# One block's residual added by GpSimd's accumulating DMAs, its norm's statistics on VectorE, and a new instruction order

## The chip, the cores and the metric

The kernel runs on one NeuronCore of a Trainium2 chip. The metric is the device time of one execution in microseconds. The profile names the engines PE (TensorE matmul), PEld (TensorE weight load), ACT (ScalarE), DVE (VectorE), POOL (GpSimd) and SP (SyncE, which only issues DMAs).

## The reference

The input is one sequence of S = 2048 positions with D = 448 features in bf16. Two layers with pre-norm residuals follow each other.

```
x = A_x
h  = x + A(layernorm(x))         # A: 16 heads of 28; each position attends to itself and
                                 #    positions 2, 4, ... 14 before it (8 taps, dilation 2), then @ wo
h2 = h + B(layernorm(h))         # B, called with y = layernorm(h):
                                 #   g  = gelu(layernorm(y) @ w1), its four 112-column groups shifted by -1, +1, -2, +2 positions
                                 #   x1 = y + g_shifted @ w2
                                 #   B  = x1 + gelu(layernorm(x1) @ w3) @ w4          # w3: 448 x 1792
```

All layer norms are without weights: (x - mean) / sqrt(var + eps).

## The kernel before, in words

The sequence is cut into 4 blocks of 512 positions (t = 0 to 3) of 4 tiles of 128 positions each. Everything stays on chip; `xin` holds the input tiles and later the sum h. The steps of a block are phases: N1 (norm of x: statistics by `bn_stats` and `bn_aggr`, a logarithm and an exponential for the power, normalization, and a small copy that doubles the last 64 columns), A1 (transposes, and q and k projections, evicted to `arena`), V (v projection to `vt`, and GpSimd DMAs that gather windows of it into `vw`), A2 (products of q and shifted k on VectorE into `qk_r`, summed by matmuls), S (softmax on VectorE and ScalarE, transposes of `pb`), A3 (VectorE spreads the weights into `bd_r`, matmuls with `vw`), O (projection with `wo`, plus the residual, into `xin`), B1 (norm of h), M (projection with w1 and GELU). The rest runs in five units u of 3, 4, 4, 4 and 1 tiles: B2 (w2 and residual), T (norm, and on GpSimd an fp32 add of `xin` to the running sum), W3 (w3 and GELU, into `h3T`), B3 (w4, last adds, output DMA from `ost`).

**The residual of O** is chosen per block by RESIDUAL (line 62, used in `phase_A3`). With 't', a fifth matmul with the identity adds the tile of `xin` in PSUM and ScalarE copies the result to `xin`; with 'v', VectorE adds PSUM to `xin`. Where STATS["B1"] (line 16) of a block is 'a', ScalarE's copy sums the row as well, and `sums_stats` has ScalarE square the four tiles; where it is 'v', `ln_stats` runs `bn_stats` and `bn_aggr` on VectorE. Block 2 (the third) has 't' and 'a'. With 'a' the identity matmul is used whatever RESIDUAL says.

**The order.** The phases first make a list of operations with their dependencies. ORDER (lines 21 to 59) is an order of all of them, written out; `schedule` (line 259) walks it. An engine's instructions are issued in the order in which they stand in ORDER, and an engine waits at a semaphore where an operation needs the result of another engine. `schedule` also has a model of times; with ORDER given, that model picks buffer slots, inserts filler matmuls into long gaps, and decides which GpSimd DMAs and which DMA transposes wait for each other. Operations marked `block` are VectorE instructions that the model holds to collide with GpSimd's.

Buffers are pools of slots: 8 PSUM banks, 2 of `qk_r`, 3 of `ost`; a new user of a slot waits for the old ones. `contract` groups projections so that the half-row matmuls of several outputs run in pairs; a pool "win" with one slot keeps these groups apart in the model.

Of the kernel before, what the change touches and what calls it, by code (L numbers as in the profile page):

```python
# [5 lines left out]
ACT = mybir.ActivationFunctionType  # L6
ALU = mybir.AluOpType
# [8 lines left out]
STATS = {'N1': 'vvva', 'B1': 'vvav', 'B2': 'aaaaa'}  # L16
# [43 lines left out]
RUNS = {'A3': '1111', 'W3': '23334'}  # L60
LOADS = '01'
RESIDUAL = 'ttvv'
# [126 lines left out]
class _Sched:  # L189
# [69 lines left out]
    def schedule(self, dma_bw=240.0, dma_fixed=2000.0, table_load=1300.0):  # L259
# [18 lines left out]
        blocked = held = entry = 0.0; waiting = None  # L278
        assert sorted(ORDER) == list(range(n))
        for idx in ORDER:  # L280
# [45 lines left out]
            else:  # L326
# [3 lines left out]
                if op.eng == "pool":  # L330
                    waiting = op if blocked > st else None
                    st = entry = max(st, blocked)
                    if op.block:
                        held = st + dur
                elif op.block:
                    if waiting is not None and st <= entry + 50.0:
                        late = st + dur - entry
                        free["pool"] += late; waiting.t1 += late; entry += late
                        for ch in children[waiting.idx]:
                            if waiting in ch.deps:  # L340
                                rdy[ch.idx] = max(rdy[ch.idx], waiting.t1 - (self.OWN if ch.eng == "pool" else 0.0))
                        if waiting.block:
                            held += late
                    else:
                        st = max(st, held)
                    blocked = st + dur
# [67 lines left out]
def bass_sequential_preLN__sliding_local_dilated__mixer_s_mlp__prompt_kernel(  # L414
# [17 lines left out]
    EPS = 1e-5  # L432
# [15 lines left out]
    with ExitStack() as es:  # L448
# [41 lines left out]
        P_win = _Pool("win", None, 1)  # L490
# [110 lines left out]
        def rstd(kind, i, m=4, summed=False, norm="v", how="p"):  # L601
# [15 lines left out]
            if how == "a":  # L617
                first = int(kind == 1)
                if not summed and (norm == "a" or kind == 1):
                    dve("tensor_scalar", 4, ns=78.0, out=nm[:, kind, i:i + m], in0=mv[:, kind, i:i + m, 0], scalar1=-1.0, scalar2=None, op0=ALU.mult)  # L620
# [511 lines left out]
```

## Time and profile before

| | us |
|---|---|
| median of 3 runs (199.99 to 200.40) | 200.25 |
| the profiled execution | 199.96 |
| span of its profile, first to last instruction | 198.2 |
| PE busy | 189.7 |
| ACT busy | 143.4 |
| DVE busy | 121.7 |
| POOL busy | 46.0 |

The span leaves out 1.76 us of the profiled execution's own time. Busy times of engines overlap, since the engines run beside each other; the granted TensorE clock was 1.00 throughout. Nearly all instructions carry one line number (that of the loop that emits them, L1090), so they are told apart by the tiles they write and read.

### The profile page before, as it was taken

The numbers are of one execution on the slowest core, as the hardware profiler recorded it, in microseconds if no ns is written. First come the engines' busy times: TensorE is split into PE (matmuls) and PEld (weight loads), VectorE is DVE, ScalarE is ACT, GpSimd is POOL, SyncE is SP. The second block draws the span as 40 slices with busy tenths as digits, with TensorE's granted clock in tenths as the row PEclk, the third lists the DMA queues.
The fourth block names the chain that finished last, engine by engine and source line by source line (L and its number), as shares of the span: only waits on it lengthen the run. The fifth ranks groups of instructions, "written<-read, shape, count | busy, mean of one in ns | idle before, by whom it ended". The sixth has DMA issues, their size and how long they took to land.

```text
span 198.2 us, 4119 instructions
## 1 busy us (share of the span) xinstructions
PE 189.7 (96%) x1667; PEld 92.6 (47%) x1667; DVE 121.7 (61%) x222; ACT 143.4 (72%) x321; POOL 46.0 (23%) x96
## 2 busy tenths in 40 slices
PE   6899999889999989999989999999999999999994
PEld 2555333443454545544545444455444455446753
DVE  5888889999989999947957775101314052310024
ACT  4849986997999999997589699991345961645300
POOL 6540199003500000036040204302050000760000
PEclk9999999999999999999999999999999999999999
DMA  5950579943995000055410410009300023210003
GB/s 160 326 162 3 107 179 224 189 88 58 237 286 198 5 3 3 10 107 126 86 20 0 80 31 3 23 0 202 102 26 0 2 40 66 73 46 0 3 0 116
DMA packets 24467, 16.81 MB, mean 85 GB/s; under 512 B 17824, under 2 KB 22880, under 8 KB 24448
## 3 DMA queue, kind: packets, MB, share of 16 engines
q1 hardware_dynamic: 22368, 9.24, 19.7%
q0 software_dynamic: 2080, 7.31, 14.8%
q8 instruction: 13, 0.21, 0.4%
q14 instruction: 6, 0.05, 0.1%
HBM read 7.91 MB, written 1.84 MB: 49 GB/s over the span
## 4 chain that ended last, share of the span: by engine, by line
PE 62%; ACT 19%; DVE 8%; DMA 5%; POOL 4%; issue 1%; SPq 0%
PE ps L1090 62%; ACT arena L1090 5%; ACT actT L1090 5%; ACT vt L1090 3%; DMA vw<-vt 3%; ACT lntm L1090 2%; DVE qk_r L1090 2%; DMA xin<-in_A_x_dram 1%; DVE lntm L1090 1%; POOL w_s L1090 1%; POOL vw L1090 1%; DVE arena L1090 1%; ACT xin L1090 1%; POOL wo_s L1090 1%; ACT L1085 1%
## 5 line engine op out<-in xcount | busy, mean ns | idle before, releaser
L1090 PE MATMUL ps<-actT,arena 128*128 128x512 bf16 (+6 forms) x404 | 71.5, 344 | 0.3 <-ACT actT L1090 0.2
L1090 PEld LDWEIGHTS ps<-actT,arena 128*128 128x128 bf16 (+1 forms) x404 | 30.7, 97 | 37.4 <-issue 6.7
L1090 PE MATMUL ps<-arena,h3T 128*128 128x448 bf16 (+1 forms) x238 | 46.4, 342 | 0.0
L1090 ACT ACTIVATE h3T<-ps 128x512 bf16<-128x512 f32 (+1 forms) x60 | 30.6, 578 | 14.0 <-PE ps L1090 13.8
L1090 ACT ACTIVATE arena<-ps 128x512 bf16<-128x512 f32 (+5 forms) x64 | 32.0, 524 | 12.0 <-PE ps L1090 11.5
L1090 DVE SCALAR_TENSOR_TENSOR ost<-ps,mrs,arena 128x448 bf16<-128x448 f32 (+1 forms) x17 | 10.9, 654 | 37.8 <-PE ps L1090 35.7
L1090 DVE TENSOR_TENSOR qk_r<-arena 128x4096 bf16<-128x4096 bf16 (+1 forms) x16 | 31.8, 2016 | 2.8 <-PE ps L1090 2.8
L1090 PEld LDWEIGHTS ps<-arena,h3T 128*128 128x128 bf16 x238 | 22.6, 98 | 19.3 <-issue 0.5
L1090 POOL DMA_DIRECT2D vw<-vt x15 | 9.0, 605 | 48.9 <-DMA actT<-lntm 48.4
L1090 DVE TENSOR_TENSOR bd_r<-arena,bmask 80x2048 bf16<-80x2048 bf16 x16 | 18.7, 1214 | 2.2 <-ACT arena L1090 2.2
L1090 POOL TENSOR_TENSOR arena<-arena,xin 128x448 f32<-128x448 f32 x16 | 16.3, 1037 | 15.2 <-ACT lntm L1090 14.5
L1090 ACT ACTIVATE actT<-ps 128x512 bf16<-128x512 f32 (+2 forms) x27 | 17.8, 679 | 2.6 <-PE ps L1090 2.4
L1090 ACT ACTIVATE lntm<-arena,nm 128x448 bf16<-128x448 f32 x16 | 10.6, 662 | 8.6 <-DVE nm L1090 8.6
L1090 POOL TENSOR_TENSOR rs_y<-rs_x,mhalf 128x4 f32<-128x4 f32 (+1 forms) x5 | 4.7, 934 | 50.1 <-DVE rs_x L1090 50.1
L1090 PE MATMUL ps<-wo_s,actT 128*128 128x448 bf16 x64 | 14.5, 354 | 1.7 <-ACT actT L1090 1.6
L1090 DVE BATCH_NORM_STATS2 st<-xin 128x6 f32<-128x448 bf16 x24 | 13.8, 610 | 1.7 <-DMA xin<-in_A_x_dram 1.6
L1090 PE MATMUL ps<-actT,w_s 128*112 128x512 bf16 (+1 forms) x64 | 14.5, 387 | 0.0
L1090 DVE SCALAR_TENSOR_TENSOR arena<-xin,rs_y,ps 128x448 f32<-128x448 bf16 x16 | 10.4, 677 | 6.7 <-PE ps L1090 6.6
L1090 PE MATMUL ps<-w_s,arena 112*128 112x448 bf16 x64 | 13.6, 352 | 0.3 <-ACT arena L1090 0.3
L1090 PE MATMUL ps<-arena,actT 128*128 128x448 bf16 (+1 forms) x64 | 12.3, 353 | 0.5 <-ACT arena L1090 0.5
L1090 PEld LDWEIGHTS ps<-actT,w_s 128*112 128x112 bf16 (+1 forms) x64 | 6.5, 128 | 6.1 <-issue 2.0
L1090 PEld LDWEIGHTS ps<-w_s,arena 112*128 112x128 bf16 x64 | 6.0, 98 | 6.3 <-ACT arena L1090 1.1
(73 smaller groups left out, 190.4 us busy)
## 6 DMA issues: line engine op xcount, KB each, us to landing
out_dram<-ost SPq DMA_DIRECT2D x15, 112.0 KB, 1.7
arena<-in_B_w_dram POOLq DMA_DIRECT2D x1, 1568.0 KB, 15.2
arena<-in_B_w_dram POOLq DMA_DIRECT2D x1, 1344.0 KB, 10.4
vw<-vt POOLq DMA_DIRECT2D x4, 320.0 KB, 5.3
vw<-vt POOLq DMA_DIRECT2D x4, 256.0 KB, 5.2
xin<-in_A_x_dram SPq DMA_DIRECT2D x2, 448.0 KB, 5.8
xin<-in_A_x_dram SPq DMA_DIRECT2D x3, 224.0 KB, 5.0
arena<-in_A_wqkv_dram SPq DMA_DIRECT2D x1, 672.0 KB, 4.8
```

The source lines that it names most:

```text
L1085: eng.preload_act_table_set("natural_log_exp_and_others")
L1090: inst = getattr(eng, meth)(**kw)
```

## The change

Four things change:
- Block 2 gets RESIDUAL 'd' and STATS 'v'. ScalarE copies the projection from PSUM to a slot of `ost` in bf16, and GpSimd issues a DMA that adds the slot to the tile of `xin`, once per tile. The identity matmul goes, ScalarE's row sums and squares go, and VectorE computes the block's statistics from `xin`.
- ORDER is replaced by another list over all operations (1104 instead of 1096).
- In `schedule` the model's DMA rate goes from 240 to 215; operations marked `block` on VectorE and GpSimd now depend on each other for real (a semaphore wait for the last such operation of the other engine, in the order of the list). More of VectorE's small instructions are marked: the shifts `nm`, the inputs `rs_x` of the powers, and the doubling copies.
- The pool "win" gets 3 slots instead of 1.

```diff
-STATS = {'N1': 'vvva', 'B1': 'vvav', 'B2': 'aaaaa'}
+STATS = {'N1': 'vvva', 'B1': 'vvvv', 'B2': 'aaaaa'}
...
-    0, 9, 8, 10, 1, 2, 3, 11, 6, 4, 35, 22, 36, 5, 37, 12, 23, 38, 13, 24, 14, 25, 39, 15, 26, 46, 16, 40, 27, 52, 17, 28, 41, 18, 53, 29, 47, 60,
-    19, 48, 30, 42, 49, 54, 20, 55, 31, 61, 66, 56, 62, 43, 21, 32, 63, 57, 67, 33, 50, 34, 68, 44, 51, 69, 64, 58, 104, 70, 105, 65, 45, 106, 107,
-    59, 72, 112, 71, 108, 73, 109, 110, 111, 144, 74, 113, 114, 75, 115, 142, 116, 122, 76, 117, 145, 124, 143, 77, 120, 78, 118, 148, 123, 79, 80,
...
+    0, 9, 7, 6, 8, 10, 1, 2, 3, 11, 4, 35, 22, 36, 37, 12, 23, 38, 13, 24, 14, 25, 39, 15, 26, 46, 16, 27, 52, 17, 28, 18, 53, 29, 55, 56, 19, 30,
+    66, 60, 20, 31, 21, 32, 61, 67, 47, 48, 33, 54, 34, 49, 50, 51, 57, 58, 62, 63, 68, 104, 105, 106, 69, 59, 64, 108, 65, 40, 107, 111, 142, 112,
+    109, 110, 70, 41, 113, 114, 42, 144, 145, 143, 71, 43, 116, 146, 115, 117, 122, 120, 148, 44, 124, 147, 149, 45, 150, 118, 125, 123, 72, 151, 73,
...
-RESIDUAL = 'ttvv'
+RESIDUAL = 'ttdv'
...
-    def schedule(self, dma_bw=240.0, dma_fixed=2000.0, table_load=1300.0):
+    def schedule(self, dma_bw=215.0, dma_fixed=2000.0, table_load=1300.0):
...
                 if op.eng == "pool":
-                    waiting = op if blocked > st else None
-                    st = entry = max(st, blocked)
                     if op.block:
-                        held = st + dur
+                        waiting = None
+                        if guard["dve"]:
+                            op.deps.add(guard["dve"]); st = max(st, guard["dve"].t1)
+                        guard["pool"] = op
+                    else:
+                        waiting = op if blocked > st else None
+                        st = entry = max(st, blocked)
                 elif op.block:
+                    if guard["pool"]:
+                        op.deps.add(guard["pool"]); st = max(st, guard["pool"].t1)
+                    guard["dve"] = op
...
-        P_win = _Pool("win", None, 1)
+        P_win = _Pool("win", None, 3)
...
-                on_pe = RESIDUAL[t] == "t" or STATS["B1"][t] == "a"
+                by_dma = RESIDUAL[t] == "d"
+                on_pe = not by_dma and (RESIDUAL[t] == "t" or STATS["B1"][t] == "a")
...
-                if on_pe:
+                if by_dma:
+                    o = _Tile(P_o)
+                    act(o(), b(lambda v: v[:, 0:D]), ACT.Copy, D)
+                    dma(lambda o=o: "res%d" % o.slot, xin[:, i, :], o(), 128 * D * 2, 600.0, "pool", accum_op=ALU.add)
+                elif on_pe:
                     act(xin[:, i, :], b(lambda v: v[:, 0:D]), ACT.Copy, D, **kw)
```

The numbers of the lists that matter at the start: block 0's tiles 0, 1, 2 and 3 have their statistics in 46, 52, 60, 66 and their aggregates in 47, 53, 61, 67; the logarithms and exponentials are 48 and 49, 55 and 56, 62 and 63, 68 and 69; tile 1's shift is 54 and 57; the normalizations are 50, 58 (on ScalarE), 64, 70 and the doubling copies 51, 59, 65, 71; the transposes of the four tiles are 104, 108, 112, 116, with filler matmuls 105, 106, 109, 110, 113, 114 between. 118 to 125 are block 0's first projections on half the width, 189 is a projection of V, 142 to 149 are the statistics and aggregates of block 1's tiles and 204 and 206 its transposes. In the new list 204 and 206 stand behind six of the projections 118 to 125 and 189; in the old list 204 stands behind all of block 0's projections.

On GpSimd's queue the new list has the four loads of wo ahead of every gather of `vw`, a load of w3 in two parts (202, 203) ahead of two of block 0's three gathers, and block 3's four gathers ahead of the four adding DMAs, without block 1's DMA transpose before them. In block 3's part of the list, the row maximum and the subtraction of its softmax (S 3) stand ahead of block 2's four normalizations, and the new statistics between the products of A2 3.

More of the change, by code (lines that the diff above doesn't have):

```diff
@@ L277, in schedule @@
         table = None
-        blocked = held = entry = 0.0; waiting = None
+        blocked = entry = 0.0; waiting = None; guard = dict(dve=None, pool=None)
         assert sorted(ORDER) == list(range(n))
@@ L341, in schedule @@
                                 rdy[ch.idx] = max(rdy[ch.idx], waiting.t1 - (self.OWN if ch.eng == "pool" else 0.0))
[L342 to L345, printed above, removed]
                     blocked = st + dur
@@ L530, in dma @@
         def dma(chan, out_ap, in_ap, nbytes, dur=450.0, eng="sp", behind=(), **kw):
-            op = S.add(eng, "dma_start", dur, 1000.0 if eng == "pool" else 0.0 if not callable(chan) else -1300.0, chan=chan, nbytes=nbytes, out=out_ap, in_=in_ap, **kw)
+            op = S.add(eng, "dma_start", dur + 100.0 * (eng == "pool"), 1000.0 if eng == "pool" else 0.0 if not callable(chan) else -1300.0, chan=chan, nbytes=nbytes, out=out_ap, in_=in_ap, **kw)
             op.odeps.update(behind)
@@ L596, in sums_stats @@
             lo, m = tiles[0], len(tiles)
-            dve("tensor_scalar", 4, ns=78.0, out=nm[:, kind, lo:lo + m], in0=mv[:, kind, lo:lo + m, 0], scalar1=-1.0 / D, scalar2=None, op0=ALU.mult)
+            dve("tensor_scalar", 4, ns=78.0, block=True, out=nm[:, kind, lo:lo + m], in0=mv[:, kind, lo:lo + m, 0], scalar1=-1.0 / D, scalar2=None, op0=ALU.mult)
             for n, i in enumerate(tiles):
@@ L619, in rstd @@
                 if not summed and (norm == "a" or kind == 1):
-                    dve("tensor_scalar", 4, ns=78.0, out=nm[:, kind, i:i + m], in0=mv[:, kind, i:i + m, 0], scalar1=-1.0, scalar2=None, op0=ALU.mult)
+                    dve("tensor_scalar", 4, ns=78.0, block=True, out=nm[:, kind, i:i + m], in0=mv[:, kind, i:i + m, 0], scalar1=-1.0, scalar2=None, op0=ALU.mult)
                 power_act(first)
@@ L629, in rstd @@
             if not summed and (norm == "a" or kind == 1):
-                dve("tensor_scalar", 4, ns=78.0, out=nm[:, kind, i:i + m], in0=mv[:, kind, i:i + m, 0], scalar1=-1.0, scalar2=None, op0=ALU.mult)
+                dve("tensor_scalar", 4, ns=78.0, block=True, out=nm[:, kind, i:i + m], in0=mv[:, kind, i:i + m, 0], scalar1=-1.0, scalar2=None, op0=ALU.mult)
             if kind == 1:
-                dve("tensor_scalar", 4, ns=78.0, out=rs_x[:, kind, 1, i:i + m], in0=var, scalar1=by * (1.0 + EPS), scalar2=EPS * EPS,
+                dve("tensor_scalar", 4, ns=78.0, block=True, out=rs_x[:, kind, 1, i:i + m], in0=var, scalar1=by * (1.0 + EPS), scalar2=EPS * EPS,
                     op0=ALU.mult, op1=ALU.add)
@@ L635, in rstd @@
             elif summed:
-                dve("tensor_scalar", 4, ns=78.0, out=rs_x[:, kind, 0, i:i + m], in0=var, scalar1=by, scalar2=EPS, op0=ALU.mult, op1=ALU.add)
+                dve("tensor_scalar", 4, ns=78.0, block=True, out=rs_x[:, kind, 0, i:i + m], in0=var, scalar1=by, scalar2=EPS, op0=ALU.mult, op1=ALU.add)
             else:
-                dve("tensor_scalar", 4, ns=78.0, out=rs_x[:, kind, 0, i:i + m], in0=var, scalar1=EPS, scalar2=None, op0=ALU.add)
+                dve("tensor_scalar", 4, ns=78.0, block=True, out=rs_x[:, kind, 0, i:i + m], in0=var, scalar1=EPS, scalar2=None, op0=ALU.add)
             if kind == 1:
@@ L641, in rstd @@
                     shifts(1)
-                dve("tensor_scalar", 4, ns=78.0, out=rs_x[:, kind, 0, i:i + m], in0=var, scalar1=by, scalar2=EPS, op0=ALU.mult, op1=ALU.add)
+                dve("tensor_scalar", 4, ns=78.0, block=True, out=rs_x[:, kind, 0, i:i + m], in0=var, scalar1=by, scalar2=EPS, op0=ALU.mult, op1=ALU.add)
             power(0)
@@ L674, in doubled @@
         def doubled(ln, lo, n):
-            dve("tensor_copy", 64, ns=142.0, out=ln(lambda v: v[:, lo:lo + n, D:512]), in_=ln(lambda v: v[:, lo:lo + n, 384:D]))
+            dve("tensor_copy", 64, ns=142.0, block=True, out=ln(lambda v: v[:, lo:lo + n, D:512]), in_=ln(lambda v: v[:, lo:lo + n, 384:D]))
         def transposed(ln, how, n=4, w=2):
```

71 rows, old and new, of the table ORDER are left out of this document.

## The prediction, made blind

> **What bounds the kernel now.** I read the page first, then the windows of 5 us, the chain of waits in order of time, TensorE's own waits, and the timeline of the first 20 us.
>
> ```profile
> PE 189.7 (96%) x1667; PEld 92.6 (47%) x1667; DVE 121.7 (61%) x222; ACT 143.4 (72%) x321; POOL 46.0 (23%) x96
> ```
>
> TensorE is busy for 189.7 of 198.2 us. It starts at 1.59 us, and its last matmul ends 2.5 us before the span does; so only 4.4 us of idle time lie inside its work. The windows (length, busy time of PE, PEld, DVE, ACT, POOL) show where:
>
> ```profile
> 5.00:10.00 5.00, 4.30 (x36) 2.59 (x35) 4.37 (x17) 4.28 (x12) 2.57 (x11) 1.00 1.09 323
> 10.00:15.00 5.00, 5.00 (x40) 2.92 (x38) 4.40 (x13) 2.49 (x8) 1.93 (x15) 1.00 0.52 156
> ...
> 35.00:40.00 5.00, 4.48 (x52) 2.18 (x53) 5.00 (x5) 4.89 (x13) 0.00 (x0) 1.00 1.02 185
> 40.00:45.00 5.00, 3.88 (x144) 2.10 (x137) 5.00 (x5) 4.86 (x13) 0.00 (x0) 1.00 0.48 95
> ...
> 70.00:75.00 5.00, 4.43 (x83) 2.02 (x81) 4.96 (x9) 4.91 (x14) 0.00 (x0) 1.00 0.01 3
> ...
> 85.00:90.00 5.00, 4.96 (x43) 2.40 (x42) 2.23 (x2) 5.00 (x16) 2.35 (x4) 1.00 0.56 104
> ...
> 100.00:105.00 5.00, 4.21 (x28) 2.14 (x27) 2.69 (x5) 4.95 (x16) 2.33 (x4) 1.00 0.00 0
> ```
>
> Idle PE: 0.70 before the first transposes, 1.64 from 35 to 45, 1.2 between 60 and 80, 0.79 at 101. Between 10 and 35 and from 105 on there is none. VectorE is nearly full from 30 to 85, ScalarE from 60 to 90: in the first half three engines run close together. The chain:
>
> ```profile
> 6.77 10.68 PE ps L1090 x88
> ...
> 87.94 3.43 DVE qk_r L1090 x2
> ...
> 100.96 0.70 DVE pb L1090
> ...
> 101.71 93.95 PE ps L1090 x664
> ```
>
> So the third block's norm lies in a stage that ends on VectorE (87.94 to 101.66), and after it TensorE alone counts. The start, which the new ORDER rearranges:
>
> ```profile
> 4.09 0.25 DVE L1090 BATCH_NORM_AGGREGATE mv<-st 128x2 f32<-128x6 f32 x2
> 4.64 0.63 DVE L1090 BATCH_NORM_STATS2 st<-xin 128x6 f32<-128x448 bf16 x1 [0.30 <-DMA xin<-in_A_x_dram]
> 6.13 0.36 DVE L1090 TENSOR_SCALAR lntm<-xin,mv,rs_y 128x448 bf16<-128x448 bf16 x1
> 6.77 0.40 PE L1090 MATMUL ps<-ident,lntm 128*128 128x128 bf16 x4 [0.70 <-DVE lntm L1090]
> 8.80 0.39 PE L1090 MATMUL ps<-ident,lntm 128*128 128x128 bf16 x4
> 9.02 5.80 PE L1090 MATMUL ps<-actT,arena 128*128 128x256 bf16 x40
> 13.61 0.21 DVE L1090 COPY lntm<-lntm 128x256 bf16<-128x256 bf16 x1
> 14.65 0.61 PE L1090 MATMUL ps<-ident,lntm 128*128 128x128 bf16 x8
> ```
>
> First transposes 6.77, fourth tile's 8.80, block 0's projections from 9.02, block 1's transposes 14.65, with no gap from 7.46 on.
>
> **Part 1, TensorE.** Four identity matmuls of 448 columns go. In the dense run at 129.27 us, 49 such matmuls take 9.43; without the last one's drain of some 0.35 that is 0.19 each: -0.76. All lie on the path. Walking both lists by the matmuls' tiling mode gives 85 changes of mode before and 86 after. One costs about 0.19: 18 full and 6 paired half matmuls at 121.48 take 4.91, where 21 x 0.216 is 4.53, for two changes. Net -0.57.
>
> **Part 2, ScalarE and VectorE.** ScalarE loses four squares (86.24 to 90.6; 0.65 apart) and eight accumulator reads of 0.20 to 0.25, about 4 us. It does not end that stage, so I count nothing. VectorE gains four statistics of 0.59 and four aggregates of some 0.12, 2.8 us. They go between the products for block 3, where VectorE waited 2.47 us for TensorE before 87.94. That idle time hides them: 0; without it, +2.8 on the VectorE chain.
>
> **Part 3, the transfers.** Four issues of 0.6 us each on GpSimd's queue (vw rows), which stood idle for 35.1 us until 87.37. Behind them on it are the norm's powers and the fp32 adds, some 10 us later. How long an adding transfer takes no row shows. Bounds: 1.7 us (112 KB to DRAM) and 5.8 (median of vw, queued); I take 3, nearer the first in size and with little else in flight. The next reader, the statistics, stands after two products of 2.3 us and block 1's norm, so up to 5.8 is hidden. Nearer is the buffer: ost has three slots, so the fourth copy on ScalarE waits for the first transfer. Between the first and the fourth copy stand one residual copy, two of actT, two of transposes and two more copies, about 4.4 us; issue and landing need 3.6. Cost 0, at the upper end +2. Just ahead of them the queue now has block 3's four window transfers, which before waited for a transpose until 87.37; their 656 KB may still be in flight, which is why 5.8 stays the bound. By the Trainium skill (DMA: Bandwidth & Descriptors, Anatomy of one DMA) a GpSimd transfer takes about 2.0 us plus bytes over 436 GB/s, an estimate of 2.3 here; by it the sum would be the same.
>
> **Part 4, explicit waits between GpSimd's adds and VectorE's small steps.** Beside two adds at 92.57 one normalization took 1.11 instead of 0.39 and one nm 0.99 instead of 0.17: the stall of 0.7 to 0.8 is there already. A semaphore in its place: 0, from -0.8 to +1.0 (one add). Queued behind a waiting VectorE step are the products and softmax steps of block 3; TensorE waits for those.
>
> **Part 5, the order at the start.** This is the term that decides. The new list puts tile 0's aggregate behind the statistics of tiles 3 and 2. They start at 4.64 with the transfer; two at 0.59, three aggregates at 0.12: 6.2 us. Logarithm and exponential (0.53) give 6.75, the normalization starts at 6.8 instead of 6.13, the first transposes at 7.4 (+0.65). ScalarE then does tile 1's shift and normalization (0.28 + 0.74) before tile 2's power: tile 2 transposes at 8.75, its fillers last until 9.8. VectorE puts a statistic of block 1 before tile 3's normalization, and another with two aggregates before its copy: 8.7 + 0.57 + 0.36 + 0.57 + 0.25 + 0.18 = 10.6, transposes at 10.7 instead of 8.80. The projections stand behind them on TensorE. Next the new list has only 18 narrow projections and one group of V (2.5 us) ahead of block 1's transposes, where the old had 5.6. TensorE reaches them at 13.5, but block 1's norm is ready at about 14.4: from 10.65, two statistics and aggregates 1.4, powers 0.53, four normalizations 1.3 to 1.6, copy 0.21. So at the same moment (14.4 against 14.65) TensorE has done 3.1 us less work: +2.8. The groups' evictions follow: the half-row matmuls that close block 0's groups end near 16.8 instead of 12.7, so ScalarE and VectorE are late too, by 2 to 3 us. On GpSimd's queue two of block 0's three window transfers move behind two parts of w3 (1.1 us of issue, 458 KB) and one transfer of block 1; their landing at 38.3 becomes 39 to 40, which the late softmax of block 0 covers; without that cover it costs 1.5.
>
> **Part 6, what gives it back.** TensorE can absorb delay only where it waited: 1.64 + 1.2 + 0.79 = 3.6 us. At 47.81 its wait ended on a transfer that does not move, worth about 1.0. The new list runs block 3's softmax ahead of block 2's normalizations, so the 0.79 at 101 should shrink, but its chain on VectorE starts late. I take 1.5 back; ends 0.5 and 3.5.
>
> **Part 7, the tail.** From block 2's projection on, the two lists hold 96.1 and 96.15 us of matmul and mode time: 0. Block 3's projection stands 2.1 us nearer to its norm, whose normalizations now precede unit 2's; 0, at worst +1.
>
> **Sum.** On the profiled execution, 199.96 (span 198.2 and 1.76 around it): -0.57 + 2.8 - 1.5 = +0.7, 200.7. The median shown is 0.29 above it: 201.0.
>
> **Rivals.**
> *The start is swallowed (faster).* All 3.5 us of later waits take up the 2.8 and the rest; -0.57 - 0.7 gives 199.0, with half of it 199.9. For: DVE and ACT have 1.3 and 2.1 us of idle time from 20 to 35. It decides if A1 3 starts before 49 us. Against: DVE stands at 4.8 to 5.0 of 5 from 30 to 85. Chance 0.30, of it 0.20 for faster.
> *Nothing is given back.* VectorE's lag of over 2 us reaches the softmax of block 3, and the new statistics lie on it: 200.25 - 0.57 + 2.8 = 202.5, with part of the 2.8 of part 2 up to 203. It decides when VectorE no longer waits before the third product of A2 3. Chance 0.09.
> *The adding transfers are slow.* Over 4 us each, the fourth copy blocks ScalarE by 2 us where it is 4.9 of 5 full: 203. Chance 0.06.
> *The clock falls back.* The first warm-up matmuls start 0.43 us apart, the later ones 0.22. TensorE's gap before the first transposes grows from 0.7 to 1.4, with two of 0.9 after it; should the slow pace return for 3.4 us, half of that is lost: 202.7. Chance 0.05. The Trainium skill (TensorE: Matmul & The Clock Gate, Part 1) has the clock halve after an idle window of about 3.4 us; by that rule these gaps are too short.
>
> **How the numbers follow.** Forecast 0.50, of it 0.04 within 0.2% of 200.25 (0.4 us, about what a measurement of this kernel can tell); swallowed start 0.20 faster and 0.10 the same; the other three 0.20 slower. That makes 0.20, 0.14 and 0.66. The forecast's own range is 200.4 to 202.0; the range to 199.0 and 203.2 takes in the first two rivals.
>
> **What would show it.** Right: first transposes near 7.4, tile 3's near 10.7, a TensorE wait before block 1's at 14.4; A1 3 at 50 to 51 instead of 47.8; no idle PE from block 2's projection on; four transfers landing in 2 to 4 us without a wait of ScalarE; VectorE's wait before 87.94 filled. Wrong: projections of block 0 still at 9; ScalarE waiting for a transfer; a TensorE wait before block 3's projection.

## The result and the profile after

The changed kernel takes 202.28 us (median of 4 runs, 202.20 to 202.42), the kernel before 200.12 beside it: a ratio of 1.0109, 95% interval 1.0085 to 1.0134. It is slower by some 2.2 us. Its profiled execution has 202.2 us and a span of 200.5, against 199.96 and 198.2. Some executions of a few kernels below ran at a lower TensorE clock; the ratios leave the slowest of them out, the medians do not, so a median and its ratio can differ.

The busy times of the changed kernel, as its profile gives them:

```profile
PE 191.2 (95%) x1670; PEld 92.9 (46%) x1670; DVE 123.6 (62%) x230; ACT 141.1 (70%) x309; POOL 51.1 (25%) x100
```

TensorE is busier by 1.5 us although four matmuls went: the fillers that the planner puts into gaps it foresees rose from 20 to 27, their busy time from 6.5 to 8.7 us, and they hide part of the new idle time. The chain of work that ended last (start, length, what):

```profile
14.64 0.63 PE ps L1099 x8
15.30 1.95 ACT actT L1099 x2
17.29 1.05 PE ps L1099 x7
...
102.51 1.46 DVE pb L1099
104.01 93.95 PE ps L1099 x664
```

The last piece is the same 93.95 us that it was before, and starts at 104.01 instead of 101.71. All of the 2.3 us lies ahead of it. TensorE's timeline at the start, with its waits in brackets:

```profile
7.27 0.40 PE L1099 MATMUL ps<-ident,lntm 128*128 128x128 bf16 x4
...
10.42 0.40 PE L1099 MATMUL ps<-ident,lntm 128*128 128x128 bf16 x4 [0.27 <-DVE lntm L1099]
10.65 2.13 PE L1099 MATMUL ps<-actT,arena 128*128 128x256 bf16 x18
...
14.64 0.62 PE L1099 MATMUL ps<-ident,lntm 128*128 128x128 bf16 x8 [0.64 <-DVE lntm L1099]
15.10 0.49 PE L1099 MATMUL ps<-actT,arena 128*128 128x256 bf16 x3
...
15.87 0.49 PE L1099 MATMUL ps<-actT,arena 128*128 128x256 bf16 x3
17.29 3.08 PE L1099 MATMUL ps<-actT,arena 64*128 64x512 bf16 x16 [0.93 <-ACT actT L1099]
```

Block 1's transposes start at the same time as before (14.64 against 14.65), but with 18 narrow projections and three matmuls of V done ahead of them instead of 40 projections, and behind them TensorE waits once more, 0.93 us, for ScalarE. In the kernel before, ten matmuls of V stood behind the first of these transposes, and TensorE did not wait there:

```profile
15.10 1.78 PE L1090 MATMUL ps<-arena,actT 128*128 128x448 bf16 x10
```

The windows of 5 us of the changed kernel (length, busy time of PE, PEld, DVE, ACT, POOL, then the granted clock, the share of DMA and GB/s):

```profile
5.00:10.00 5.00, 4.65 (x28) 2.05 (x26) 3.71 (x14) 3.68 (x11) 0.71 (x3) 1.00 1.09 332
10.00:15.00 5.00, 4.08 (x36) 2.85 (x36) 4.35 (x14) 1.10 (x3) 4.12 (x23) 1.00 0.51 154
15.00:20.00 5.00, 4.07 (x35) 2.15 (x33) 3.82 (x13) 3.92 (x9) 0.00 (x0) 1.00 0.01 3
...
85.00:90.00 5.00, 5.00 (x44) 2.52 (x43) 4.64 (x9) 4.21 (x9) 0.58 (x1) 1.00 0.91 153
```

Between 10 and 20, where there was no gap, TensorE now idles for 1.85 us, and ScalarE does 1.10 of 5 us from 10 to 15. From 85 to 90 VectorE has 4.64 instead of 2.23. Only part of that is the new statistics: two of the four lie in its old wait ahead of the third product, which is now 0.33 us long instead of 2.47, and the other two stand around the fourth product. The rest is work that comes later than before.

```profile
88.38 1.14 DVE L1099 BATCH_NORM_STATS2 st<-xin 128x6 f32<-128x448 bf16 x2
89.85 2.29 DVE L1099 TENSOR_TENSOR qk_r<-arena 128x4096 bf16<-128x4096 bf16 x1 [0.33 <-PE ps L1099]
```

A measure that needs no window is the start of the matmuls that transpose each block's softmax result (`ps<-ident,pb`, eight for each block): fillers apart, both kernels have the same number of matmuls ahead of each, until the four identity matmuls are missing at block 3. All runs, in us; the time is the median of each run, the points are those of one execution, whose own time stands in the column "profiled":

| kernel | time | ratio to before | profiled | block 0 | block 1 | block 2 | block 3 |
|---|---|---|---|---|---|---|---|
| before | 200.0 to 200.2 | 1 | 199.96 | 36.20 | 57.69 | 68.61 | 101.71 |
| after | 202.28 | 1.0109 (1.0085 to 1.0134) | 202.20 | 40.43 | 61.42 | 72.12 | 104.01 |
| old_first_half | 204.56 | 1.0187 (1.0151 to 1.0222) | 206.94 | 36.19 | 59.26 | 77.03 | 108.75 |
| new_first_half | 203.52 | 1.0175 (1.0162 to 1.0188) | 203.50 | 40.64 | 61.63 | 72.31 | 105.32 |
| residual_alone | 200.85 | 1.0042 (1.0027 to 1.0057) | 201.14 | 36.39 | 57.88 | 68.81 | 102.50 |
| residual_undone | 203.03 | 1.0155 (1.0141 to 1.0168) | 202.97 | 40.46 | 61.44 | 72.17 | 104.77 |
| planner_only | 200.37 | 1.0007 (0.9986 to 1.0029) | 200.57 | 36.77 | 58.47 | 69.39 | 102.40 |
| old_to_310 | 200.02 | 0.9992 (0.9970 to 1.0014) | 199.84 | 36.75 | 58.92 | 69.72 | 101.62 |
| old_to_219 | 200.52 | 1.0010 (0.9982 to 1.0037) | 202.06 | 37.26 | 61.19 | 71.99 | 103.88 |
| softmax_first | 199.26 | 0.9950 (0.9932 to 0.9969) | 199.47 | 36.37 | 57.78 | 68.70 | 101.07 |
| softmax_first_only | 199.25 | 0.9937 (0.9907 to 0.9968) | 199.12 | 36.47 | 57.86 | 68.78 | 100.92 |
| first_norm_old | 200.88 | 1.0031 (1.0007 to 1.0054) | 200.81 | 39.02 | 60.00 | 70.71 | 102.63 |
| adds_behind_pb | 202.27 | 1.0103 (1.0080 to 1.0127) | 202.24 | 40.47 | 61.45 | 72.16 | 104.05 |
| plain_copy | 202.18, one run | none | 202.18 | 40.45 | 61.43 | 72.14 | 104.00 |

After against before, the lag is 4.23, 3.73, 3.51 and 2.30 us. It is made before 40 us and shrinks slowly; 0.76 of it goes with the identity matmuls between the third and the fourth point.

Small differences between points need care, because executions of the same list begin differently. With the old list at the start the first transposes came at 6.77 in before, 6.95 in residual_alone, 7.10 in softmax_first_only and 7.40 in planner_only, and block 0's point is later by nearly the same amount (0, 0.19, 0.27, 0.57; planner_only has one filler more there). So a lag of up to 0.6 us can be the start of that execution and not the list. The new list takes most of this up in its waits at the start: first transposes at 7.27, 7.50 and 7.72 in after, residual_undone and new_first_half, block 1's transposes at 14.64, 14.67 and 14.85.

### The profile page after: what moved, and what is told of

Same layout as the page of the kernel before. It is cut to its first block, busy times and chain, and to the rows that moved or that the text cites. A ratio compares the mean times of both kernels' runs of the same rounds, so it can differ in the third digit from the quotient of the medians.

```text
span 200.5 us, 4125 instructions
## 1 busy us (share of the span) xinstructions
PE 191.2 (95%) x1670; PEld 92.9 (46%) x1670; DVE 123.6 (62%) x230; ACT 141.1 (70%) x309; POOL 51.1 (25%) x100
## 4 chain that ended last, share of the span: by engine, by line
PE 62%; DVE 18%; ACT 15%; DMA 1%; issue 1%; SPq 0%
PE ps L1099 62%; ACT arena L1099 6%; DVE bd_r L1099 5%; DVE qk_r L1099 4%; DVE lntm L1099 3%; DVE st L1099 3%; ACT actT L1099 3%; ACT lntm L1099 2%; DMA xin<-in_A_x_dram 1%; DVE zs L1099 1%; DVE pb L1099 1%; ACT vt L1099 1%; ACT L1094 1%; ACT L1099 1%; ACT rs_x L1099 1%
## 5 line engine op out<-in xcount | busy, mean ns | idle before, releaser
L1099 PE MATMUL ps<-arena,h3T 128*128 128x448 bf16 (+1 forms) x238 | 46.9, 342 | 0.0
L1099 DVE BATCH_NORM_STATS2 st<-xin 128x6 f32<-128x448 bf16 x28 | 16.2, 613 | 0.8 <-DMA xin<-in_A_x_dram 0.6
L1099 PE MATMUL ps<-arena,actT 128*128 128x448 bf16 (+1 forms) x64 | 12.8, 353 | 0.6 <-ACT arena L1099 0.6
L1099 POOL TENSOR_TENSOR rs_y<-rs_x,mhalf 128x4 f32<-128x4 f32 (+1 forms) x5 | 5.6, 1112 | 27.6 <-DVE nm L1099 15.9
L1099 DVE COPY lntm<-lntm 128x256 bf16<-128x256 bf16 (+2 forms) x16 | 3.7, 228 | 13.5 <-ACT lntm L1099 13.2
L1099 PE MATMUL ps<-ident 128*128 128x512 bf16 x27 | 8.7, 471 | 1.6 <-POOL epsilon L1099 1.6
## 6 DMA issues: line engine op xcount, KB each, us to landing
arena<-in_B_w_dram POOLq DMA_DIRECT2D x1, 1344.0 KB, 10.7
```

Of the source, the lines that this page charges most:

```text
L1099: inst = getattr(eng, meth)(**kw)
```

## The experiments

The theory was that the new ORDER's start loses the time; the rival, that the residual and its statistics cost it. Four kernels were built to cross the two.

**old_first_half**: the changed kernel with the old order for the first half.

```diff
 ORDER = [
-    0, 9, 7, 6, 8, 10, 1, 2, 3, 11, 4, 35, 22, 36, 37, 12,
+    0, 9, 8, 10, 1, 2, 3, 11, 6, 4, 35, 22, 36, 5, 37, 12,
...
```

> The changed kernel, with the first 385 entries of its ORDER put back into the order of the kernel before (the two lists have done the same operations there but one; this is about the first 50 us). Residual, statistics, planner and the second half of the list stay as changed. Theory 'the start loses it': the third block's first group of Q and K (A1 3) starts near 47.8 us again instead of 52.0, and the time falls below the kernel before: 199.5 us if the 1.9 us that came back behind 52 us were only idle time that took up the delay, 198.1 if the new second half is itself that much shorter. Rival 'the residual and its statistics cost it': 201.5 to 202.3.

Measured 204.56 us (six executions, 202.87 to 206.94), slower than either kernel, against both expectations. The start was as before (36.19), and then the cut made a fault of its own. ScalarE's and TensorE's timelines and windows of 2 us (columns as above):

```profile
66.28 0.54 ACT L1099 ACTIVATE vt<-ps 128x448 bf16<-128x448 f32 x1 [3.76 <-DMA vw<-vt]
```

```profile
70.25 4.66 PE L1099 MATMUL ps<-w_s,arena 112*128 112x448 bf16 x12 [3.98 <-ACT arena L1099]
```

```profile
68.00:70.00 2.00, 0.00 (x0) 0.00 (x0) 0.06 (x1) 1.99 (x5) 0.00 (x0) 0.77 0.00 0
70.00:72.00 2.00, 1.75 (x5) 0.72 (x6) 0.00 (x0) 1.97 (x3) 0.00 (x0) 0.50 0.00 0
```

A window transfer of block 2 is the last of its four on GpSimd's queue in the old list, behind two loads of weights (1568 and 1344 KB), and the first in the new one; block 3's last copy of V, which waits for it, comes late in the old list and early in the new one. The mixture had the old transfer and the new copy, so ScalarE stood for 3.76 us in front of the evictions that TensorE needed, and TensorE's clock fell to a half. Its time tells nothing on the theory.

**new_first_half**: the kernel before with the changed planner and, for the first 385 entries, the changed order (the same diff the other way, residual and statistics as before).

> The kernel before with the changed planner, and with the first 385 entries of ORDER in the changed order; residual by identity matmuls, statistics on ScalarE, the second half of the list as before. Theory 'the start loses it': A1 3 starts near 52 us, 202.3 to 204.3 us by how much of 4.2 us the old second half can take up (3.6 us of TensorE idle time lay there, I expect about 1.5 to be given back: 203). Rival 'the residual and its statistics cost it': 200.1 to 200.6.

203.52 us, ratio 1.0175: the new first half, with the changed planner, makes 3.5 us by itself, with a lag of 4.44 at block 0 and 3.61 at block 3. Theory, and the upper half of its range: less came back than I thought.

**residual_alone**: the kernel before with its own list.

```diff
-STATS = {'N1': 'vvva', 'B1': 'vvav', 'B2': 'aaaaa'}
+STATS = {'N1': 'vvva', 'B1': 'vvvv', 'B2': 'aaaaa'}
-RESIDUAL = 'ttvv'
+RESIDUAL = 'ttdv'
...
+                if by_dma:
+                    o = _Tile(P_o)
+                    act(o(), b(lambda v: v[:, 0:D]), ACT.Copy, D)
+                    dma(lambda o=o: "res%d" % o.slot, xin[:, i, :], o(), 128 * D * 2, 600.0, "pool", accum_op=ALU.add)
```

> The kernel before, its planner and its ORDER, with only the third block's residual on adding transfers and its four statistics on VectorE; each transfer stands right behind its copy, three statistics ahead of the third product of A2 3 and the fourth between it and the next. Theory 'the start loses it': four identity matmuls less, the statistics in VectorE's 2.5 us wait: 199.5 to 200.1 us. Rival 'the residual and its statistics cost it': 201.5 to 202.5, with VectorE's chain to the softmax of the fourth block late by 1 to 3 us.

200.85 us, ratio 1.0042: slower by 0.84, between the two. Two of TensorE's waits: the one for the fourth product is new, the one ahead of block 3's transposes was 0.79 before. Then what VectorE did ahead of the fourth product:

```profile
92.21 1.05 PE L1096 MATMUL ps<-qk_r,zc 128*32 128x512 bf16 x16 [0.48 <-DVE qk_r L1096]
...
102.50 0.64 PE L1096 MATMUL ps<-ident,pb 128*80 128x128 bf16 x8 [1.18 <-DVE pb L1096]
```

```profile
89.99 0.62 DVE L1096 BATCH_NORM_STATS2 st<-xin 128x6 f32<-128x448 bf16 x1
90.65 0.18 DVE L1096 BATCH_NORM_AGGREGATE mv<-st 128x2 f32<-128x6 f32 x1
```

Three statistics lie in VectorE's old wait, as forecast; the fourth stands between the third product and the fourth, delays the fourth, and with it block 3's softmax. A third wait of TensorE also grew, at 78.84, from 0.20 to 0.61, for ScalarE.

**residual_undone**: the changed kernel with the lines above put back (identity matmuls, squares on ScalarE in the places of the statistics).

> The changed kernel with only the residual and the statistics of the third block as before (identity matmuls, sums and squares on ScalarE; the squares stand where the four statistics stood). Theory 'the start loses it': 202.3 to 203.2 us, the start as late as in the changed kernel. Rival 'the residual and its statistics cost it': 200 to 200.6.

203.03 us: in the new list the residual and its statistics gain 0.75, and the lag at block 3 without them is 3.06 instead of 2.30. The difference of 0.76 is what the four identity matmuls were priced at. So the residual and its statistics are no cause of the loss.

**planner_only**: the kernel before with only the planner's code changed (explicit waits, three slots, 215 for 240).

> The kernel before with its own ORDER, residual and statistics; only the planner's code is the changed one (explicit waits between GpSimd's adds and VectorE's small steps, three slots for the window transfers, 215 instead of 240 bytes per ns in its model of the transfers). Theory 'the list decides, not the planner': 199.8 to 200.4 us. Rival 'the explicit waits cost it': 200.6 to 201.2, with VectorE's steps near 92 us and from 101 on waiting for GpSimd.

200.37 us, ratio 1.0007 (0.9986 to 1.0029): with the old list the planner's code makes no difference that can be measured. The new list was not run with the old planner, so this run does not exclude a cost of the planner there. The next two and first_norm_old have the changed planner and differ from the changed kernel in the list alone.

**old_to_310**: as old_first_half, with the cut at 309 entries, ahead of the transfer.

> The changed kernel with the first 309 entries of ORDER in the order of before; the cut is moved ahead of the window transfer that in the run old_first_half stood behind w4's load and held ScalarE for 3.8 us and TensorE for 4.0. Theory 'the start loses it': A1 3 at 47.8 to 49 us, no such wait, 198.5 to 199.6 us. Rival 'the new second half cannot be fed by the old start': 200.5 to 202, with a wait of TensorE of over 1 us between 50 and 80.

200.02 us, ratio 0.9992 against 1.0109: some 2.3 us come back, the whole loss. It lies between the two expectations (198.5 to 199.6, 200.5 to 202). From block 0's point to block 3's it takes 64.87 us, against 65.51 before, when the four matmuls alone are 0.76. The stretches differ: between blocks 0 and 1, where the two lists meet, it loses 0.68; from block 2 to block 3 it takes 31.90, against 33.10 before and 31.89 in the changed kernel. So the new list's last stretch is as short behind the old start as behind its own, and the place where the lists meet cost about what the new order gave.

**old_to_219**: only the first 219 entries, to about 24 us.

> The changed kernel with only the first 219 entries of ORDER in the order of before: this reaches to about 24 us. Theory 'the loss is made by 24 us' (3.6 of the 4.2 us were there when block 0's first zc matmuls began): first transposes at 6.8, tile 3's at 8.8, block 0's first zc matmuls near 23.8, A1 3 near 48.5, 198.7 to 200.0 us. Rival 'the loss comes from how blocks 1 and 2 are ordered between 24 and 48 us': 201 to 202.3, with A1 3 at 50 or later.

200.52 us, ratio 1.0010, between the two expectations. At block 0 the lag is 1.06 instead of 4.23, so most of the loss is made before 24 us. In the profiled execution (202.06, the longest of twelve) 2.4 us more is lost between blocks 0 and 1 (23.93 us instead of 21.49), with TensorE's clock at a half behind a wait of 1.60:

```profile
42.78 0.42 PE L1099 MATMUL ps<-bd_r,vw 80*32 80x64 bf16 x32 [1.60 <-ACT vt L1099]
...
44.35 1.67 PE L1099 MATMUL ps<-wo_s,actT 128*128 128x448 bf16 x4
```

```profile
42.00:44.00 2.00, 1.22 (x51) 0.71 (x55) 1.53 (x2) 1.77 (x4) 0.00 (x0) 0.96 0.13 26
44.00:46.00 2.00, 2.00 (x37) 0.83 (x25) 2.00 (x2) 1.91 (x6) 0.00 (x0) 0.50 1.12 213
```

**first_norm_old**: only block 0's normalization and transposes in the old order, about 9 us; this divides the start.

> The changed kernel with only block 0's normalization and transposes in the order of before (the list up to the copy of tile 3's transposed tile, about the first 9 us); behind it everything as changed, so block 1's transposes still have only 18 narrow projections and one group of V ahead of them. First transposes at 6.8, tile 3's at 8.8. Theory 'the loss is made by the first norm and passed on': block 1's norm is ready 1.6 to 1.9 us earlier, its transposes near 12.9, 200.4 to 200.8 us. Rival 'the loss is made by the thin work ahead of block 1's transposes': they stay near 14 us, TensorE waits before them, and the time is 201.6 to 202.3.

200.88 us, 1.40 less than the changed kernel and just above the 200.4 to 200.8 expected. TensorE at block 1:

```profile
13.47 0.61 PE L1099 MATMUL ps<-ident,lntm 128*128 128x128 bf16 x8
...
16.11 3.08 PE L1099 MATMUL ps<-actT,arena 64*128 64x512 bf16 x16 [0.93 <-ACT actT L1099]
```

Block 1's transposes came 1.17 earlier, not 1.7, and everything behind them 1.4 earlier to the end. So of the lag of 4.23 the first norm's order makes 1.41. The other 2.82 is what is left; I put it down to the thin work ahead of block 1's transposes and the wait of 0.93 behind them, which is unchanged here, but no run changes these two alone. Some 0.26 of it may be the later start of this execution (first transposes at 7.03 against 6.77). The rival's wait ahead of block 1's transposes did not appear; eight fillers stand there.

**softmax_first**: residual_alone with two moves on VectorE: the fourth statistic behind the fourth product, and block 3's row maximum and subtraction (560, 561) ahead of block 2's normalizations (539 to 543).

```diff
...
-531, 532, 533, 558, ..., 534, ..., 541, 474, 539, ..., 542, 540, ..., 543, ..., 560, ..., 561
+558, 531, 532, 533, ..., 534, ..., 560, 561, 541, 474, 539, ..., 542, 540, ..., 543, ...
...
```

> The run residual_alone with two moves on VectorE, as the changed list has them: the fourth statistic behind the fourth product of A2 3 instead of ahead of it, and the fourth block's two first softmax steps ahead of the third block's normalizations. Theory 'the residual costs 0.84 in the old list only because its chain is in front of that softmax': TensorE's waits of 0.48 at 92 us and 1.18 at 102.5 both go to under 0.3 and the time falls to 199.0 to 199.7 us, under the kernel before. Rival 'the transfers and statistics cost by themselves': 200.4 to 200.9, with the wait before the fourth block's transposes of over 0.8 us still there.

199.26 us, ratio 0.9950 (0.9932 to 0.9969): faster than both kernels, as expected. The wait at 92 us is gone; that ahead of block 3's transposes fell to 0.41, not to under 0.3.

**softmax_first_only**: the kernel before with the second of these moves alone, and nothing of the change.

> The kernel before with one change of its list: the fourth block's two first softmax steps ahead of the third block's normalizations; residual by identity matmuls, statistics on ScalarE. It says what of softmax_first's gain belongs to the residual. Theory 'the residual is worth its four matmuls once its chain is off the softmax': TensorE's wait of 0.79 at 101.7 us goes, 199.3 to 199.7, and softmax_first is 0.3 to 0.8 us faster still. Rival 'the gain is the softmax alone': 198.9 to 199.2, no slower than softmax_first.

199.25 us, ratio 0.9937 (0.9907 to 0.9968), the same as softmax_first. The rival was right (its range ended at 199.2): the gain is the softmax's place. The four matmuls that softmax_first saves came back as waits. TensorE in softmax_first, then in softmax_first_only:

```profile
78.74 4.45 PE L1096 MATMUL ps<-actT,arena 128*128 128x384 bf16 x28 [0.62 <-ACT actT L1096]
...
101.07 0.64 PE L1096 MATMUL ps<-ident,pb 128*80 128x128 bf16 x8 [0.41 <-DVE pb L1096]
```

```profile
78.81 4.50 PE L1090 MATMUL ps<-actT,arena 128*128 128x384 bf16 x28 [0.19 <-ACT actT L1090]
...
100.92 0.61 PE L1090 MATMUL ps<-ident,pb 128*80 128x128 bf16 x8
```

Three of the four matmuls stand ahead of a place where TensorE waits for ScalarE anyhow (78.7 to 78.8 in both), and at block 3's point VectorE is last: 0.43 and 0.41 more of waiting, 0.84 for the 0.76 saved.

**adds_behind_pb**: the changed kernel with the first of GpSimd's three fp32 adds (418) moved behind the product pb (565) in the list; the other two (417, 416) stood behind it already.

```diff
...
-563, 418, 564, ..., 565, ..., 417, 479, 416
+563, 564, ..., 565, 418, ..., 417, 479, 416
...
```

> The changed kernel with the three fp32 adds of GpSimd that start at 101.4 us moved behind the fourth block's last softmax product (pb), which took 1.45 us beside them instead of 0.70; TensorE waited 0.43 us for it. Theory 'VectorE's product is stretched by the adds': pb takes 0.7 us, that wait is gone, 201.7 to 202.0 us. Rival 'the product is slow by itself or the wait has another cause': 202.2 to 202.4.

202.27 us, nothing changed, and the run decides nothing: the list orders each engine's own queue, GpSimd's was empty, and the adds still started at 101.41, beside pb with 1.45. The stretching can only be read across kernels: pb takes 1.45 or 1.46 in the eight whose adds run beside it, all with the new list at that place (after, this one and six others), and 0.69 in the six without (before, residual_alone, softmax_first, softmax_first_only, planner_only, new_first_half).

**plain_copy**: the changed kernel without `accum_op=ALU.add`, so that the four transfers overwrite the tiles of `xin`.

> The changed kernel with the four transfers copying instead of adding: it leaves out the third block's residual, and is there for the landing time alone. Theory 'adding costs nothing above a copy': the four land in 2.9 to 3.8 us as in the changed kernel, whole time 202.2. Rival 'adding makes them slower': they land in under 2.3 us; the whole time stays, since nobody waited for them.

The landing times (min, median, max) of the changed kernel, then of this one:

```profile
DMA to landing us min/median/max: 2.9/3.1/3.8
```

```profile
DMA to landing us min/median/max: 1.9/2.1/3.8
```

Adding costs 1.0 us in the median of four transfers. The time stays (202.18, one execution): nobody waited for them.

## Why the prediction was right, and where its sum was off

The mechanism forecast decides: the order at the start, with TensorE alone behind block 3. The time, 202.28 against 201.0, came out above the forecast's own range of 200.4 to 202.0, inside the wider one. A rise of 0.75 us was forecast and one of 2.16 measured, so the direction and the mechanism were right and the size was not: part 5 was too small by 1.4 us. The nearest number in the prediction is that of the rival "nothing is given back" (202.5), but by chance: its condition, that VectorE no longer waits before the third product, did not hold (0.33 us were left), and 1.17 us was given back. It comes near because two of its terms miss in opposite ways: 2.8 where 4.23 was measured, and nothing given back.

- **Part 1** (-0.57): the four matmuls were worth 0.76 in the new list (residual_undone). The 0.19 for one more change of mode was not tested: both kernels of that comparison have the new list. In a list where VectorE is last at block 3's point the four matmuls were worth nothing.
- **Part 2** (0): right for the new list. VectorE's 2.47 us of waiting shrank to 0.33, in part because two of the statistics lie in it. The condition named there ("without it, +2.8") held in part in residual_alone, where one statistic of four was not hidden.
- **Part 3** (0): landing 2.9 to 3.8 us with 3 taken, no wait of ScalarE. The issues took 1.06 each in the median, not 0.6; GpSimd had room for that. (The four window transfers add up to 640 KB, not 656; nothing hangs on it.)
- **Part 4** (0): planner_only gives 1.0007, with the old list. In the changed kernel the adds' stall moved from the normalization onto pb, and TensorE waited 0.43 us for pb. That 0.43 is the most that the stall can have cost; the run meant to take it away left it in place, so this stays open.
- **Part 5** (+2.8) is the term that was mis-sized, by 1.4; 4.23 is measured at block 0's point. Its steps were right to 0.3 us: 7.27, 10.42 and 14.64, where 7.4, 10.7 and 14.4 were forecast. The sum ended at block 1's transposes. Behind them the new list has only six narrow matmuls to cover ScalarE's two copies of 0.97 (15.30 to 17.24), where the old list had ten projections of V (1.78 us): TensorE waits 0.93 and then 0.17. With 3.1 us of work missing at 14.64 that makes 4.2. The half-row matmuls did not end at 16.8 but at 20.4. The gap of 1.4 us that was feared ahead of the first transposes did not come: fillers covered it.
- **Part 6** (-1.5): 4.23 less 0.76 less 2.30 leaves 1.17 given back. first_norm_old gives 2.82 less 0.76 less 0.92, 1.14. From two different lags the same amount came back. That alone would also fit waits that take up a fixed amount of any large lag. But in the old list a late start was not taken up: planner_only is 0.57 late at block 0's point and 0.69 at block 3's. So the 1.17 is most likely the new list's own, and not idle time that grew smaller because TensorE came later. Some 0.7 comes back by block 2 in every kernel with the new first half (new_first_half 0.50 and 0.24); from block 2 to block 3, residual_undone gives back 0.50 and new_first_half 0.09, and these two differ only in the second half of the list. The single wait named in part 6, at 47.81 and worth about 1.0, was misread: TensorE was busy for 1.98 of the 2 us from 46 to 48 there. The rival of a swallowed start fell here: A1 3 began at 52.0, its condition was under 49; the forecast's own sign, 50 to 51, was missed as well. (That rival's 199.9 does not come out of its own terms.)
- **Part 7** (0): exact, 93.95 us in both.

With the measured sizes the sum is -0.76 + 4.23 - 1.17 = 2.3, the shift of the last piece of the chain. The 1.17 is what the other numbers leave, so that the sum closes is no proof of it. Of the other rivals, slow adding transfers fell with the landing times of part 3, and a clock that falls back with the granted clock of 1.00 at the start.

## What to carry to other kernels

When an edit comes with a newly computed order, price the order first and its own edit second: here the edit was worth -0.75 us in one list, nothing in a second and +0.84 in a third. Follow a delay past the first instruction that was late to the next place where the engine has too little other work, and count only such waits as taken up whose releasing engine is not late as well. On a stage that ends on another engine, moving two short steps of that engine's chain forward (softmax_first_only, 0.9 us) was worth more than taking work off the busiest engine.

## What the runs showed of the hardware

- A transfer that adds to its target took 3.1 us from issue to landing against 2.1 for a copy of the same 112 KB in the same place, and its issue held GpSimd's queue for 1.06 us against 0.55 (medians of four each, after and plain_copy).
- The clock can fall after much shorter waits than I allowed for. In old_to_219 it went to a half at 43.8 us, behind waits of 0.46, 0.55 and 1.60 us between 37.9 and 42.8; it then stayed there for 3.4 us, and four matmuls took 1.67 instead of 0.93. In before, waits of 0.86 and 0.26 at 41.6 and 44.8 left it at 1.00, and in the changed kernel so did waits of 0.64 and 0.93 between 14.00 and 17.29, 1.57 us together. So no limit on the idle time comes out of these traces. The Trainium skill (TensorE: Matmul & The Clock Gate, Part 1) tells of a fall after an idle window of about 3.4 us; the duration agrees with this trace, the idle time does not. That the gaps at the start of the changed kernel left the clock at 1.00 agrees with it.
- Beside GpSimd's fp32 adds, VectorE's product of two SBUF tiles (pb) took 1.45 us instead of 0.69 (eight kernels against six), while the row sum (0.68) and the reciprocal (0.55) just ahead of it kept their times. The Trainium skill (SBUF — State Buffer, Who interferes with whom) says that a VectorE instruction with two SBUF inputs contends with a GpSimd instruction that reads SBUF; the trace agrees.
